# Moving the query casts of batches 2 to 7 from VectorE to GpSimd in a fused attention and feed-forward kernel

## The chip, the core and the metric

The kernel runs on one core of a Trainium2 chip. A core has TensorE (PE, matrix products), VectorE (DVE), ScalarE (ACT), GpSimd (POOL) and SyncE (SP). Each of them works through a queue of its own, in order, and waits on semaphores for the others. DMAs are issued from the queues of SP, POOL and ACT. The metric is the device time of one execution in microseconds (us), median over the runs.

## What is computed

A sliding-window attention (each position sees those at a distance of at most 32), then a feed-forward layer with the tanh form of GELU. The inputs are float32, 8 batches, 8 heads, 576 positions, 64 numbers per head; the feed-forward layer takes 4608 tokens of 512 numbers to 2048 and back.

```python
scores = scale * np.matmul(q, k.transpose(0, 1, 3, 2))
mask = np.abs(pos[:, None] - pos[None, :]) <= window
attn = softmax(np.where(mask, scores, -1e9))
x = (attn @ v).transpose(0, 2, 1, 3).reshape(B * S, H * D)
h = x @ w_in
out = gelu_tanh(h) @ w_out
```

(The softmax and the GELU are written out in the reference; they are named here to keep it short.)

## The kernel before

The attention of batch b and the feed-forward layer of the token tile t = b - 1 (512 tokens, nine tiles) run woven into each other. One tile goes like this. PE first computes the hidden columns: 16 columns of four 128x512 products each (`ffn_in`, L446), ScalarE applies the GELU to each (L454), and VectorE forms sums of them after every fourth column (`sums`, L487), since the second product is done with a scheme of seven block products for eight. Then PE runs the 112 products of the second layer (`ffn_out`, L542). Between these, at positions written by hand in the table `PLAN`, stand the steps of the attention of batch b: `s` is a score group (L354), one for each of the four head pairs and one for the tail positions; `m` the mask (VectorE, L369); `v` the weighting with V (L387); `x` the spreading of the result into the token buffer xT (VectorE, L411 and L417). The first score group stands after the sixth L542 product, the second after the 24th. PE takes all this in that order, without passing a step that waits.

The scheduling is by hand: each engine gets its instructions in the order in which the program emits them.

Queries and keys come as float32 with positions in rows, and the scores need them as float16 with the 64 numbers of a head in the partitions. For batches 0 and 1 this is done on PE. For batches 2 to 7, in the tiles t = 1 to 6, `cast_and_turn` does it, at the end of the first columns of the tile: VectorE casts the queries (`queries`, L310, four casts of 128x512, one per head pair) and SP issues one transposing DMA for them (L313, into QT); then for each head pair VectorE casts the keys (L318) and SP issues a transposing DMA (L319, into KT); then the same for the last 64 positions (L310 on 16 partitions and L313; L323 and L324). SP then issues the loads of the next batch's queries and keys (`load_qk`, L160 to L165). A score group of head pair p reads the whole of QT's pair p and KT's pair p.

GpSimd, in these tiles, only issues DMAs: the loads of V with a cast to float16 (`load_v`, L170 and L172: for batch 2 at the end of tile 0, for batch b + 1 behind the first `v` step in tile t), and the stores of the output rows (`store`, L503). Of a tile's stores, four are emitted after block product 5 (VectorE's L571) and seven in `ffn_last`, after VectorE's L580. `ffn_last` of a tile comes ahead of `cast_and_turn` of the next in the program.

The buffers that the change touches: the loaded queries `qr` (two), their tails `qt` (one), the casts `q16` and `qt16` (one each), QT and KT (two each).

Of the kernel before, what the change touches and what calls it, by code (L numbers as in the profile page):

```python
# [61 lines left out]
def kernel(  # L62
# [9 lines left out]
    nc = tc.nc  # L72
# [173 lines left out]
    def cast_open(b):  # L246
        halfs[b] = [hp.tile([128, NPAIR, 4, 2, 64], FP16, name="q16"),
                    hp.tile([128, NPAIR, 4, 2, 64], FP16, name="k16")]
        QTs[b] = ap_.tile([128, NPAIR, 4, 144], FP16, name="QT")
# [52 lines left out]
    def cast_and_turn(b):  # L302
        cast_open(b)
        q16, k16 = halfs[b]
        qr, kr, qt, kt = raws[b]
        qt16 = hp.tile([16, NPAIR, 4, 2, 64], FP16, name="qt16")
        kt16 = hp.tile([64, NPAIR, 2, 64], FP16, name="kt16")
        def queries(src, dst, p0, p1):
            for pr in range(NPAIR):
                nc.vector.tensor_copy(  # L310
                    dst[:, pr, :, :, :].rearrange("p j h d -> p h j d"),
                    src[:, 2 * pr:2 * pr + 2, :].rearrange("p h (j d) -> p h j d", j=4))
            nc.sync.dma_start_transpose(QTs[b].rearrange("d r j p -> d (r j) p")[:, :, p0:p1],  # L313
                                        dst.rearrange("p r j h d -> p (r j h d)"))

        queries(qr, q16, 0, 128)
        for pr in range(NPAIR):
            nc.vector.tensor_copy(k16[:, pr, :, :, :], kr[:, :, 2 * pr:2 * pr + 2, :])  # L318
            nc.sync.dma_start_transpose(  # L319
                KTs[b % 2][:, pr, 0:512].rearrange("d (c p) -> d c p", c=4),  # L320
                k16[:, pr, :, :, :].rearrange("p c h d -> p (c h d)"))
        queries(qt, qt16, 128, 144)
        nc.vector.tensor_copy(kt16.rearrange("p r h d -> p (r h d)"), kt.rearrange("p h d -> p (h d)"))  # L323
        nc.sync.dma_start_transpose(  # L324
            KTs[b % 2][:, :, 512:576], kt16.rearrange("p r h d -> p (r h d)"))
# [464 lines left out]
```

## Time and profile before

| What | Value |
|---|---|
| Median of 11 runs | 312.18 us (311.0 to 313.34) |
| The profiled execution | 311.7 us, its span 309.8 us |
| PE busy | 297.4 us (96%) |
| DVE busy | 198.4 us (64%) |
| ACT busy | 199.9 us (65%) |
| POOL busy | 102.2 us (33%) |
| Granted TensorE clock | 0.998 |

The span goes from the first to the last instruction in the trace; the execution's time has some 1.9 us around it. A row of a group of instructions gives line, engine, operation, what is written and read, shapes and count; behind the bar the busy time in us, the mean of one in ns, and the idle time of the engine just before, with what ended it. A row of a timeline gives start and length in us, engine, line and count; in brackets the idle time before and what ended it. "SPq" is SP's queue: the length there is that of issuing, and the data land later.

### The profile page before, as it was taken

To read this page: it belongs to the slowest core of one execution; us is meant where nothing else is said; L and a number is where in the kernel's file an instruction comes from. 1 tells how busy PE (TensorE), PEld (TensorE's weight loads), DVE (VectorE), ACT (ScalarE), POOL (GpSimd) and SP (SyncE) were. 2 spreads that over 40 slices of the span, in tenths; PEclk is the share of its full clock that TensorE was granted. 3 is DMA by queue.
4 is the path that set the end of the run, shared out by engine and by line. 5 is a ranking of instruction groups with operands and counts; after the bars stand their busy time and mean duration, and the time that the engine had idled before them with its cause. 6 is when DMAs were issued, how large, how long until landed. Compare 5 with 4: busy or idle time off the path is not lost.

```text
span 309.8 us, 6732 instructions
## 1 busy us (share of the span) xinstructions
PE 297.4 (96%) x2643; PEld 187.2 (60%) x2643; DVE 198.4 (64%) x453; ACT 199.9 (65%) x315; POOL 102.2 (33%) x158
## 2 busy tenths in 40 slices
PE   7888999999899999999999999999999999999993
PEld 2453545446684588548854785478647764784583
DVE  5763586669969477947785678666866643632451
ACT  1786477578577786768676777677768676706600
POOL 3557355192019210921094108510710061006000
PEclk9999999999999999999999999999999999999999
DMA  7999999999997998899779995999392022004013
GB/s 206 259 357 367 376 333 229 261 175 149 187 201 177 154 220 128 138 173 233 140 161 136 255 132 126 171 224 161 90 159 44 2 69 69 2 0 136 2 36 100
DMA packets 120061, 50.64 MB, mean 163 GB/s; under 512 B 101327, under 2 KB 113359, under 8 KB 120030
## 3 DMA queue, kind: packets, MB, share of 16 engines
q1 hardware_dynamic: 84329, 37.50, 58.9%
q0 software_dynamic: 34768, 11.54, 30.7%
q10 hardware_dynamic: 933, 1.18, 1.1%
q8 instruction: 20, 0.33, 0.5%
q14 instruction: 11, 0.09, 0.1%
HBM read 37.62 MB, written 9.44 MB: 152 GB/s over the span
## 4 chain that ended last, share of the span: by engine, by line
PE 71%; SPq 11%; DMA 11%; DVE 4%; issue 1%; POOL 0%; DVEq 0%
PE mm L542 30%; PE mm L446 20%; PE ph L446 12%; SPq L139 5%; PE ps_o L387 4%; DMA wst<-in_moe_w_in_dram 3%; PE ps_s L354 3%; DMA qr<-in_q_dram 3%; PE ps_d L387 2%; DMA KT<-k 2%; SPq L162 2%; DMA kr<-in_k_dram 2%; SPq L130 1%; SPq L185 1%; SPq L181 1%
## 5 line engine op out<-in xcount | busy, mean ns | idle before, releaser
L446 PEld LDWEIGHTS <-w_in 128*128 128x128 f16 x576 | 56.0, 98 | 66.4 <-POOL w_in L190 1.2
L446 PE MATMUL mm<-xT,w_in 128*128 128x512 f16 x352 | 86.3, 379 | 0.6 <-DVE xT L411 0.6
L503 POOL DMA_DIRECT2D out_dram<-y x77 | 45.2, 594 | 116.1 <-DVE y L571 115.4
L454 ACT ACTIVATE gT<-mm 128x512 f16<-128x512 f32 x88 | 52.4, 599 | 36.6 <-PE mm L446 36.6
L446 PE MATMUL ph<-xT,w_in 128*128 128x512 f16 x224 | 58.6, 379 | 0.3 <-POOL w_in L190 0.2
L487 DVE TENSOR_TENSOR s<-gT 128x512 f16<-128x512 f16 x64 | 26.9, 420 | 41.2 <-ACT gT L454 41.2
L542 PEld LDWEIGHTS <-s 128*128 128x128 f16 x512 | 48.6, 98 | 7.5
L360 ACT ACTIVATE pe<-ps_s 128x704 f16<-128x704 f32 x64 | 43.3, 727 | 9.1 <-PE ps_s L354 9.0
L542 PE MATMUL mm<-t,s 128*128 128x256 f16 x376 | 45.7, 273 | 0.0
L401 ACT ACTIVATE lt<-ps_d 128x480 f32<-128x480 f32 (+3 forms) x40 | 22.2, 556 | 31.0 <-PE ps_d L387 30.9
L454 ACT ACTIVATE gT<-ph 128x512 f16<-128x512 f32 x56 | 33.0, 599 | 13.8 <-PE ph L446 13.8
L542 PEld LDWEIGHTS <-gT 128*128 128x128 f16 x384 | 36.0, 98 | 7.3
L542 PE MATMUL mm<-w_out,gT 128*128 128x256 f16 x256 | 32.8, 273 | 0.0
L369 DVE TENSOR_TENSOR pe<-pe,mask 128x704 f16<-128x704 f16 x64 | 31.0, 521 | 1.7 <-ACT pe L360 1.5
L411 DVE TENSOR_TENSOR xT<-ps_o,lt 128x480 f16<-128x480 f32 (+5 forms) x38 | 20.2, 549 | 13.7 <-ACT lt L402 13.7
L387 PEld LDWEIGHTS <-V 128*64 128x64 f16 x336 | 17.9, 109 | 11.3 <-issue 4.7
L402 ACT ACTIVATE lt<-lt 128x480 f32<-128x480 f32 (+3 forms) x40 | 23.5, 587 | 1.3
L387 PE MATMUL ps_o<-pe,V 128*64 128x160 f16 (+2 forms) x244 | 21.8, 241 | 1.3 <-DMA V<-in_v_dram 0.7
L87 ACT ACT_TABLE_LOAD x17 | 21.8, 1283 | 1.1 <-PEq L774 0.8
L387 PE MATMUL ps_d<-pe,ones 128*64 128x192 f16 (+2 forms) x264 | 22.3, 235 | 0.0
L170 POOL DMA_DIRECT2D V<-in_v_dram x24 | 21.9, 940 | 0.0
L354 PE MATMUL ps_s<-QT,KT 64*128 64x192 f16 (+5 forms) x336 | 17.9, 227 | 1.2 <-DVE KT L290 1.1
(79 smaller groups left out, 296.2 us busy)
## 6 DMA issues: line engine op xcount, KB each, us to landing
kr<-in_k_dram SPq DMA_DIRECT2D x32, 256.0 KB, 6.8
qr<-in_q_dram SPq DMA_DIRECT2D x6, 1024.0 KB, 7.5
V<-in_v_dram POOLq DMA_DIRECT2D x30, 128.0 KB, 8.0
wst<-in_moe_w_in_dram SPq DMA_DIRECT2D x3, 1024.0 KB, 8.3
wst<-in_moe_w_out_dram SPq DMA_DIRECT2D x3, 1024.0 KB
qr<-in_q_dram SPq DMA_DIRECT2D x8, 256.0 KB
vr<-in_v_dram SPq DMA_DIRECT2D x16, 128.0 KB, 7.6
out_dram<-y POOLq DMA_DIRECT2D x24, 48.0 KB, 2.4
```

What stands on the lines that cost most here:

```text
L170: nc.gpsimd.dma_start(V[:, c, :, :], v[b, :, 128 * c:128 * c + 128, :].rearrange("h p d -> p h d"))
L354: nc.tensor.matmul(ps[:, h, off:off + 4 * n].rearrange("k (j p) -> k j p", j=4), KTs[b % 2][r0:r0 + 64, pr, k0:k0 + 128], QTs[b][r0:r0 + 6 ...
L360: nc.scalar.activation(pe, ps[:, :, 0:w], AF.Exp, scale=SCALE)
L369: nc.vector.tensor_tensor(pe, pe, m.rearrange("p (o w) -> p o w", o=1).broadcast_to(list(pe.shape)), op=ALU.mult)
L387: nc.tensor.matmul(bk[r0:r0 + 64, at:at + 4 * n].rearrange("d (j p) -> d j p", j=4)[:, :, p0 - q0:p1 - q0], V[:, c, 2 * pr + h, :] if w == ...
L401: nc.scalar.activation(lt[:, 0:n], d[:, 0:n], AF.Ln)
L402: nc.scalar.activation(lt[:, 0:n], lt[:, 0:n], AF.Exp, scale=-1.0)
L446: nc.tensor.matmul(ph, w_in16[:, dc, fc * 128:fc * 128 + 128], xT[:, dc, t * 512 % RING:t * 512 % RING + 512], start=(dc == 0), stop=(dc = ...
L454: nc.scalar.activation(gTs[t][:, fc, :], phs[fc], AF.Gelu_apprx_tanh)
L487: nc.vector.tensor_tensor(dst, x, y, op=op)
L503: (eng or turn_about[0] if t == NT - 1 else eng or nc.gpsimd).dma_start(out_v[b, j, q0 + p:q0 + p + e, cols], yo[m:m + e, cols])
L542: nc.tensor.matmul(pys["apart"][:, 0:256] if apart else py[:, blk, :], lhsT, wino[w][:, f, :], start=(new and i % (8 if one else 16) == 0) ...
```

## The change

In `cast_and_turn` the casts of the queries, those of the 512 first positions and those of the last 64, are emitted for GpSimd. The keys stay on VectorE. Nothing else is changed, and the order of the program is the same.

```diff
         def queries(src, dst, p0, p1):
             for pr in range(NPAIR):
-                nc.vector.tensor_copy(
+                nc.gpsimd.tensor_copy(
                     dst[:, pr, :, :, :].rearrange("p j h d -> p h j d"),
                     src[:, 2 * pr:2 * pr + 2, :].rearrange("p h (j d) -> p h j d", j=4))
             nc.sync.dma_start_transpose(QTs[b].rearrange("d r j p -> d (r j) p")[:, :, p0:p1],
                                         dst.rearrange("p r j h d -> p (r j h d)"))
```

It is called twice in each of six tiles, with four casts each time: 48 casts.

## The prediction, made before the change was built

> **What bounds the kernel now.** I read the page's busy shares first, then the time windows by stage, then the timelines of GpSimd (POOL), SyncE (SP) and TensorE (PE) around one batch change. The windows, one per token tile:
>
> ```profile
> core 0: us, PE busy (x) PEld busy (x) DVE busy (x) ACT busy (x) POOL busy (x), PEclk, DMA share, GB/s
> 60.00:93.00 33.00, 31.95 (x297) 20.82 (x296) 27.42 (x57) 23.04 (x38) 11.62 (x14) 1.00 1.54 179
> 93.00:125.00 32.00, 32.00 (x299) 20.97 (x298) 22.23 (x53) 23.57 (x38) 11.36 (x17) 1.00 1.20 167
> 188.70:220.50 31.80, 31.80 (x297) 20.83 (x296) 22.06 (x52) 23.37 (x38) 11.23 (x17) 1.00 1.12 164
> ```
>
> First column: length of the window; then busy time by engine. TensorE is busy in the whole of the tiles t = 2 to 6 and waits for nobody there. VectorE has about 10 us to spare in each. Only tile 1 (60 to 93 us) has holes in PE. So relief for VectorE is worth something in tile 1 alone, and anything that makes PE wait is paid in full.
>
> The groups of instructions give the price of the cast on each engine:
>
> ```profile
> L310 DVE CAST qt<-qt 16x512 f16<-16x512 f32 x24 | 9.2, 438 | 0.0
> L310 DVE CAST q<-qr 128x512 f16<-128x512 f32 x24 | 8.7, 423 | 0.0
> L253 POOL CAST q<-qr 128x512 f16<-128x512 f32 x7 | 4.5, 650 | 4.7 <-DMA qr<-in_q_dram 4.6
> ```
>
> The 48 casts that move are 17.9 us of VectorE time; the same shape took GpSimd 650 ns in the prologue.
>
> The timeline of GpSimd at the two batch changes that matter (start, length, line, count):
>
> ```profile
> 62.00 3.59 POOL L170 DMA_DIRECT2D V<-in_v_dram  x4
> 65.53 1.13 POOL L172 DMA_DIRECT2D V<-in_v_dram  x1
> ...
> 91.68 2.17 POOL L503 DMA_DIRECT2D out_dram<-y  x4 [14.72 <-DVE y L571]
> 94.09 4.53 POOL L503 DMA_DIRECT2D out_dram<-y  x7 [0.25 <-DVE y L580]
> 98.62 3.61 POOL L170 DMA_DIRECT2D V<-in_v_dram  x4
> ```
>
> That of SP, and PE's first two score groups of batch 3:
>
> ```profile
> 62.30 4.41 SPq L313 DMA_TRANSPOSE QT<-q  x1
> 66.81 6.32 SPq L319 DMA_TRANSPOSE KT<-k  x4
> ...
> 95.57 2.79 SPq L313 DMA_TRANSPOSE QT<-q  x1
> 98.46 6.57 SPq L319 DMA_TRANSPOSE KT<-k  x4
> ```
>
> ```profile
> 107.61 0.47 PE L354 MATMUL ps_s<-QT,KT 64*128 64x160 f16 x8
> ```
>
> What to see: GpSimd is not idle when the casts are due. It issues the eleven output stores of the tile just ended, the last seven only after VectorE's L580, and is done at 98.62; VectorE has finished the query casts at 95.5. The transpose of the queries (L313) heads SP's queue, and those of the keys (L319) stand behind it.
>
> **Part one: what is removed.** 24 x 423 + 24 x 438 ns = 20.7 us counted by means, 17.9 us busy without overlaps. In tiles 2 to 6 this is worth nothing (PE 32.00 of 32.00). In tile 1 the output stage, from PE's first L542 (73.80) to the next tile's first L446 (93.05), lasts 19.25 us against 17.99 in tile 2 (106.86 to 124.85). The 1.3 us difference are three waits: 0.32 for KT, 0.66 at 80.78 (the profile puts it down to a V load, but the spread L417 that frees the same PSUM bank ended at 80.63 on VectorE), 0.36 for xT. VectorE is busy without a break from 64.6 to 85; the tail casts leaving take 2.1 us out of that (those of qr end before a 2.4 us wait for kr and save nothing). Credit: 1.3 us at most, once.
>
> **Part two: how late the query transpose becomes.** GpSimd takes its queue in the order of the program: stores of the old tile, then the eight casts, then the V loads of the next batch. Tiles 2 to 6: stores end 3.05 us after today's issue of L313 (98.62 against 95.57; in the others 3.04, 3.05, 3.04, 3.05). The stores may get quicker: eleven took 6.7 to 6.8 us where VectorE casts beside them and 5.68 at 250.76, where it doesn't, so 0.516 each against 0.647 for the seven at 94.09. With 2.8 of 4.5 us of casts gone, 7 x 0.131 x 0.62 = 0.57 us. Then four casts: 4 x 0.65 = 2.6, and 0.07 for the semaphore, as today. Delay = 3.05 - 0.57 + 2.67 = 5.15 us. Bounds: 5.0 (casts at 0.613, the shortest usual) to 6.0 (stores no quicker, 0.72 as L190's on GpSimd).
>
> Here a rule of the Trainium skill bears on the price ("SBUF — State Buffer", section Terms): VectorE in a two-port mode and GpSimd take a shared port pair as an exclusive lock, and the loser blocks for a whole instruction. By it each of the four casts could wait for one of VectorE's sums (0.42 us), 1.7 us more. The row nearest, L190, has GpSimd at 0.71 to 0.72 beside busy VectorE against 0.61 alone: 0.1 per cast. I take the row; the rule's extra is in the upper end.
>
> Tile 1 is different: ahead of the casts stand the five V loads of batch 2, until 66.66. Delay = 66.66 + 2.67 - 62.30 = 7.03 us.
>
> **Part three: how much of that is covered.** From today's issue of L313 to score group 0 (it needs the queries and key pair 0) are 12.04 us in tile 2, and to group 1 (110.54) 14.97; in the other tiles 12.0 to 12.4 and 15.0 to 15.3. After the change 6.9 and 9.8 are left, in tile 1 5.3 and 8.3. The trace's DMA completion counts say when key pair 0 landed after the issue of L313: 12.3, 9.05, 9.84, 9.16, 8.75, 9.36 us in tiles 1 to 6; key pair 1: 13.5, 12.8, 13.0, 12.2, 10.9, 9.6. None fits. PE takes its queue in order, so it stands at the score group with all of L542 behind it.
>
> What these latencies will be is the main unknown. Upper end: as now, tile by tile. Then PE waits for the later of the two pairs, 3.0, 3.1, 2.3, 1.9, 2.4 us in tiles 2 to 6, and 7.0 in tile 1. Lower end: today the stores' packets run among the transposes, and after the change they are gone by then; the quickest query transpose landed 5.7 us after issue (tile 4), one key pair is 1.3 us more (the spacing on SP), so 7.0 and 8.3: PE waits 0.1 a tile and 1.7 in tile 1. I take the nearest undisturbed row, tile 5's 8.75 and 10.9 for all, because V loads (issued 2.6 us after L313 then, 3.05 now) still collide with the key transposes. Tiles 2 to 6: 8.75 - 6.9 = 1.86 each, 9.3 together; pair 1 (10.9 - 9.8 = 1.1) is then already paid. Tile 1: 8.75 - 5.3 = 3.4, less the credit of 1.3: 2.1.
>
> The other things moved: the four tail casts run behind the first four on GpSimd, ready before SP has issued the keys: nothing. V loads come some 5 us later; batch 3's landed by 82.8 and are read after 110: nothing. The next batch's q and k loads follow the transposes on SP and also slip by 5; the last key block landed at 93.5 for a cast at 95.4, so VectorE's key casts of batch 3 may wait some 2 us with the sums (L487) behind them, but the transpose of these keys stands behind that of the queries anyway: nothing, in later tiles the margin is over 5 us.
>
> Sum: 9.3 + 2.1 = 11.4 us. The profiled execution took 311.7 us (span 309.8), so 323.1; it lies 0.5 below the median of the runs, 312.18, which gives **323.6 us**.
>
> A second rule, "TensorE: Matmul & The Clock Gate", Part 1: after about 3.4 us without work PE's clock halves, and needs as long to come back. The row: PEclk is 9 in every slice, and the longest wait of PE in the trace is 1.3 us, so no row shows it. At 1.9 us a tile it costs nothing; with the upper end's 7.0 us in tile 1 it would add 1.7 us.
>
> **Rivals.** (a) The whole delay is passed on, latencies as today: 12.7 + 7.0 - 1.3 = 18.4, with the cold spell 20.1: 330.6 to 332.3. For it: the six latencies are measured with the same V loads; against it: the stores leave. Chance 0.2. (b) Transposes near their quickest: 0.5 + 0.4, up to 6 us: 313.1 to 318. For it: key pairs of tile 6, without V loads, landed 0.2 to 1.3 us apart. Chance 0.2. (c) Not slower: the transposes hide it all and VectorE's relief in tile 1 is kept. That decides at a latency of 6.9 us for pair 0 (5.3 in tile 1), against 8.75 at best today: 312.2 - 1.3 = 310.9. Chance 0.1, half of it within 0.3%. It is also what comes if GpSimd is given the casts ahead of the stores: then the delay is 4 x 0.23 = 0.9 us and lies within the 2 to 4 us of slack; but today's order on GpSimd is the program's. The forecast, 319 to 327: 0.5.
>
> About 0.3% (0.9 us) is what a measurement can tell from no change. Slower 0.9, same 0.05, faster 0.05. The range 314 to 332 leaves out (c) and the far end of (a).
>
> **What would show it.** Right: L313's transposes issue some 5 us later against the end of the stores' tile, after a GpSimd cast; PE has a wait of about 2 us before L354 in each of tiles 1 to 6, put down to KT or QT, none elsewhere; tiles lengthen from 31.8 to about 33.7; VectorE's busy time falls by 18 us and GpSimd's rises by about 31. Wrong: L313 issued before the stores; no wait at L354; waits of PE on s or xT, which would mean that port contention slows the sums instead.

## The result and the profile after

The changed kernel takes 317.14 us in the median of 12 runs (314.71 to 319.35), against 312.17 us of the kernel before; the ratio is 1.0157, with a 95% interval of 1.0137 to 1.0178. It is slower by 5.0 us. The forecast was 323.6, an increase of 11.4: the sign was right and the range holds the time, but the size is less than half of what was forecast.

The profiled execution took 317.17 us (span 315.5, against 309.8). Its windows, one per tile, cut where the tiles now begin:

```profile
core 0: us, PE busy (x) PEld busy (x) DVE busy (x) ACT busy (x) POOL busy (x), PEclk, DMA share, GB/s
61.30:98.00 36.70, 33.46 (x298) 21.74 (x297) 28.06 (x49) 23.23 (x38) 18.83 (x22) 0.95 1.43 159
98.00:130.60 32.60, 31.88 (x299) 20.82 (x297) 23.05 (x45) 23.50 (x38) 16.02 (x25) 1.00 1.24 163
194.20:226.00 31.80, 31.80 (x298) 20.78 (x297) 23.26 (x45) 23.38 (x38) 16.12 (x25) 1.00 1.11 166
```

Tile 1 now lasts 36.7 us with 3.2 us of holes in PE, and the granted clock falls to 0.95 in it; tile 2 lost 0.7 us. The tile at 194 us is as long as it was, and PE is busy in all of it. So the forecast wait of "about 2 us before L354 in each of tiles 1 to 6" came in tile 1, a little of it in tile 2, and nowhere else. PE's timeline at the first score group of batches 2, 3 and 4 (in brackets the wait):

```profile
78.79 0.74 PE L354 MATMUL ps_s<-QT,KT 64*128 64x160 f16 x8 [2.88 <-DMA KT<-k]
...
113.32 0.46 PE L354 MATMUL ps_s<-QT,KT 64*128 64x160 f16 x8 [0.72 <-DMA KT<-k]
...
145.12 0.47 PE L354 MATMUL ps_s<-QT,KT 64*128 64x160 f16 x8
```

GpSimd and SP at the two batch changes that the prediction shows:

```profile
66.74 0.94 POOL L172 DMA_DIRECT2D V<-in_v_dram  x1
67.61 4.96 POOL L310 CAST q<-qr 128x512 f16<-128x512 f32 x4
72.52 3.04 POOL L310 CAST qt<-qt 16x512 f16<-16x512 f32 x4
...
99.01 3.94 POOL L503 DMA_DIRECT2D out_dram<-y  x7 [0.24 <-DVE y L580]
102.94 2.48 POOL L310 CAST q<-qr 128x512 f16<-128x512 f32 x4
105.38 3.04 POOL L310 CAST qt<-qt 16x512 f16<-16x512 f32 x4
```

```profile
72.60 1.81 SPq L313 DMA_TRANSPOSE QT<-q  x1
74.51 1.87 SPq L319 DMA_TRANSPOSE KT<-k  x1
...
105.45 1.99 SPq L313 DMA_TRANSPOSE QT<-q  x1
107.54 1.65 SPq L319 DMA_TRANSPOSE KT<-k  x1
```

The casts stand behind the V loads in tile 1 and behind the stores in tile 2, and L313 is issued just after the fourth, as forecast. New to see: in tile 1 the four casts took 4.96 us, twice as long as in tile 2.

Where the 5.7 us of span went is read from PE's timeline, by the length of the second layer's stage (from the first L542 of a tile to the first L446 of the next). I call it the stage below. In tile 1 it lies between these rows, in the kernel before and then after:

```profile
73.80 0.82 PE L542 MATMUL mm<-w_out,gT 128*128 128x256 f16 x6
93.05 0.81 PE L446 MATMUL mm<-xT,w_in 128*128 128x512 f16 x3
```

```profile
75.09 0.82 PE L542 MATMUL mm<-w_out,gT 128*128 128x256 f16 x6
97.96 0.81 PE L446 MATMUL mm<-xT,w_in 128*128 128x512 f16 x3
```

| | tile 1 begins | stage of tile 1 | of tile 2 | of tiles 3 to 6 |
|---|---|---|---|---|
| before | 59.99 | 19.25 | 17.99 | 17.99 to 18.05 |
| after | 61.27 | 22.87 | 18.78 | 17.99 to 18.05 |

3.62 us in tile 1, 0.79 in tile 2, and 1.28 ahead of tile 1, where the programs are the same. The last I take for drift of the prologue from one execution to the next: tile 1 began between 60.1 and 61.5 in every kernel below, whether or not its casts had moved, and the 59.99 of before is the earliest of all. The part of the change in this trace is 4.4 us.

### The profile page after: what moved, and what is told of

Same layout as the page of the kernel before. It is cut to its first block, busy times and chain, and to the rows that moved or that the text cites. A ratio compares the mean times of both kernels' runs of the same rounds, so it can differ in the third digit from the quotient of the medians.

```text
span 315.5 us, 6732 instructions
## 1 busy us (share of the span) xinstructions
PE 300.0 (95%) x2643; PEld 188.5 (60%) x2643; DVE 205.1 (65%) x405; ACT 200.3 (64%) x315; POOL 134.9 (43%) x206
## 4 chain that ended last, share of the span: by engine, by line
PE 68%; DMA 13%; SPq 10%; DVE 6%; issue 1%; POOL 0%; ACT 0%; DVEq 0%
PE mm L542 30%; PE mm L446 17%; PE ph L446 10%; SPq L139 4%; PE ps_o L387 4%; PE ps_s L354 3%; DMA KT<-k 3%; DMA wst<-in_moe_w_in_dram 3%; DMA qr<-in_q_dram 3%; PE ps_d L387 3%; DVE s L487 2%; SPq L162 2%; DMA kr<-in_k_dram 2%; DMA vr<-in_v_dram 2%; DVE k L318 1%; SPq L181 1%
## 5 line engine op out<-in xcount | busy, mean ns | idle before, releaser
L446 PEld LDWEIGHTS <-w_in 128*128 128x128 f16 x576 | 56.0, 98 | 65.5 <-POOL w_in L190 0.7
L503 POOL DMA_DIRECT2D out_dram<-y x77 | 42.2, 555 | 111.2 <-DVE y L571 110.5
L446 PE MATMUL mm<-xT,w_in 128*128 128x512 f16 x352 | 86.3, 379 | 0.1
L446 PE MATMUL ph<-xT,w_in 128*128 128x512 f16 x224 | 58.5, 379 | 0.1
L487 DVE TENSOR_TENSOR s<-gT 128x512 f16<-128x512 f16 x64 | 34.7, 542 | 36.0 <-ACT gT L454 35.8
L542 PEld LDWEIGHTS <-s 128*128 128x128 f16 x512 | 48.6, 98 | 7.5
L542 PE MATMUL mm<-t,s 128*128 128x256 f16 x376 | 45.7, 273 | 0.0
L542 PEld LDWEIGHTS <-gT 128*128 128x128 f16 x384 | 36.4, 99 | 7.8
L542 PE MATMUL mm<-w_out,gT 128*128 128x256 f16 x256 | 33.7, 278 | 0.0
L369 DVE TENSOR_TENSOR pe<-pe,mask 128x704 f16<-128x704 f16 x64 | 32.1, 539 | 1.1 <-ACT pe L360 1.1
L387 PEld LDWEIGHTS <-V 128*64 128x64 f16 x336 | 18.3, 110 | 12.4 <-issue 5.8
L487 DVE TENSOR_TENSOR s<-s,gT 128x512 f16<-128x512 f16 x32 | 22.7, 710 | 1.1
L387 PE MATMUL ps_o<-pe,V 128*64 128x160 f16 (+2 forms) x244 | 21.7, 241 | 1.7 <-DVE pe L369 0.7
L354 PE MATMUL ps_s<-QT,KT 64*128 64x192 f16 (+5 forms) x336 | 18.2, 229 | 4.3 <-DMA KT<-k 3.6
L387 PE MATMUL ps_d<-pe,ones 128*64 128x192 f16 (+2 forms) x264 | 22.2, 235 | 0.0
```

Of the source, the lines that this page charges most:

```text
L354: nc.tensor.matmul(ps[:, h, off:off + 4 * n].rearrange("k (j p) -> k j p", j=4), KTs[b % 2][r0:r0 + 64, pr, k0:k0 + 128], QTs[b][r0:r0 + 6 ...
L369: nc.vector.tensor_tensor(pe, pe, m.rearrange("p (o w) -> p o w", o=1).broadcast_to(list(pe.shape)), op=ALU.mult)
L387: nc.tensor.matmul(bk[r0:r0 + 64, at:at + 4 * n].rearrange("d (j p) -> d j p", j=4)[:, :, p0 - q0:p1 - q0], V[:, c, 2 * pr + h, :] if w == ...
L446: nc.tensor.matmul(ph, w_in16[:, dc, fc * 128:fc * 128 + 128], xT[:, dc, t * 512 % RING:t * 512 % RING + 512], start=(dc == 0), stop=(dc = ...
L487: nc.vector.tensor_tensor(dst, x, y, op=op)
L503: (eng or turn_about[0] if t == NT - 1 else eng or nc.gpsimd).dma_start(out_v[b, j, q0 + p:q0 + p + e, cols], yo[m:m + e, cols])
```

## The experiments

Theory A: the whole loss is the wait for the transposes in tile 1 (with the slow clock that follows it), and a bit in tile 2; in tiles 3 to 6 the transposes land so much sooner after their issue that the delay is hidden. Theory B: the casts on GpSimd slow VectorE's sums by contention, in every tile alike. For B speaks the group of the sums on VectorE, here before and then after:

```profile
L487 DVE TENSOR_TENSOR s<-s,gT 128x512 f16<-128x512 f16 x32 | 13.6, 425 | 1.1
```

```profile
L487 DVE TENSOR_TENSOR s<-s,gT 128x512 f16<-128x512 f16 x32 | 22.7, 710 | 1.1
```

The stages in the profiles of all kernels, with the medians:

| kernel | median us | ratio to before, interval | stage of tile 1 | of tile 2 |
|---|---|---|---|---|
| from batch 3 on GpSimd | 313.02 | 1.0027 (1.0008 to 1.0047) | 18.72 | 18.19 |
| batch 2 alone on GpSimd | 316.25 | 1.0117 (1.0088 to 1.0146) | 23.61 | 17.99 |
| idle products | 315.76 | 1.0107 (1.0068 to 1.0145) | 21.47 | 17.99 |
| V loads behind the casts | 312.61 | 0.9999 (0.9977 to 1.0020) | 18.46 | 18.12 |
| stores behind the casts | 315.81 | 1.0104 (1.0065 to 1.0142) | 22.67 | 17.99 |
| long sums later | 314.55 | 1.0071 (1.0049 to 1.0093) | 20.31 | 19.15 |
| all early | 316.06 | 1.0118 (1.0090 to 1.0146) | 22.53 | 17.99 |
| batch 2 early | 315.66 | 1.0091 (1.0058 to 1.0123) | 22.29 | 17.99 |
| batch 2 early, V behind | 311.68 | 0.9980 (0.9967 to 0.9994) | 19.06 | 17.99 |
| all on GpSimd, V behind | 312.96 | 1.0016 (0.9999 to 1.0033) | 18.46 | 18.87 |
| seven stores left out | 313.79, one run | | 21.18 | 17.99 |
| no DMAs of GpSimd there | 312.98, one run | | 19.60 | 17.99 |

**Which batch costs it.** Two kernels halve the change:

```diff
-                nc.gpsimd.tensor_copy(
+                (nc.gpsimd if b > 2 else nc.vector).tensor_copy(
```

> Batch 2's query casts stay on VectorE, those of batches 3 to 7 are on GpSimd. Theory A (the loss is the wait for the transposes in tile 1, 3.6 us of it, and 0.8 in tile 2, while tiles 3 to 6 hide the delay): the time is that of before plus 0 to 0.9 us, 312.2 to 313.1, and TensorE has no wait over 0.8 us at L354. Theory B (port contention: VectorE's sums, 542 and 710 ns against 420, slow every tile alike): five sixths of the 5.0 us stay, about 316.3.

```diff
-                nc.gpsimd.tensor_copy(
+                (nc.gpsimd if b == 2 else nc.vector).tensor_copy(
```

> Only batch 2's query casts are on GpSimd. Theory A: the 3.6 us of tile 1 stay, and as the next loads slip, up to 0.8 more: 315.5 to 316.6; the clock drops to half for 3.4 us after the wait. Theory B: one sixth stays, about 313.0.

313.02 and 316.25, both where theory A has them. Five of six batches on GpSimd cost 0.7 us (in the profile 0.2 in the stage of tile 2 and 0.4 in that of tile 5), the one batch of tile 1 costs 3.9. Theory B falls: the sums are slower by the row above, but nobody waits for them, as VectorE had the time to spare. (In these tiles of after PE has three waits over 0.15 us: the two at L354, and 0.36 for xT, which before has too.)

**What the slow clock costs.** In the changed kernel the granted clock is halved in one stretch, from 78.6 to 82.0 us, right behind the wait in tile 1. The windows of that stretch (the three numbers at the end are PEclk, the DMA share and GB/s):

```profile
75.10:78.60 3.50, 0.81 (x7) 0.48 (x5) 3.43 (x9) 1.88 (x2) 3.50 (x5) 1.00 1.14 152
78.60:82.00 3.40, 3.21 (x33) 2.35 (x34) 1.27 (x4) 2.26 (x4) 1.30 (x2) 0.51 2.05 170
```

```diff
                 elif kind == "s":
+                    if t == 1 and g == 0:
+                        spin(14, 512)
                     score(*group(g))
```

> As after, with 14 idle products of 512 columns (3.0 us) on TensorE just ahead of the first score group of tile 1, into a spare bank, which compute nothing that is used. Theory A with the slow clock: they fill the wait, the granted clock stays at full, and the 3.4 us at half clock, worth up to 1.7 us, fall away: about 315.5. If the clock costs nothing: 317.1 or a little more.

315.76: 1.4 us less than after, and the stage of tile 1 is also 1.4 us shorter (22.87 to 21.47). The clock is full there:

```profile
75.30:79.00 3.70, 3.70 (x21) 1.85 (x19) 3.63 (x10) 1.88 (x2) 3.70 (x5) 1.00 0.74 86
79.00:83.00 4.00, 4.00 (x57) 3.17 (x57) 3.51 (x8) 2.90 (x5) 1.09 (x2) 1.00 2.15 157
```

But the products did not fill a wait here. In this execution the keys arrived later, VectorE's long sums (L471) therefore began behind the query casts, and the four casts took 3.03 us instead of 4.96:

```profile
67.80 3.03 POOL L310 CAST q<-qr 128x512 f16<-128x512 f32 x4
71.03 1.20 DVE L471 TENSOR_TENSOR t<-w_out 128x2048 f16<-128x2048 f16 x1
75.94 3.19 PE L215 MATMUL spin<-KT 128*128 128x512 f16 x14
```

Key pair 0 had landed at 75.9, about when score group 0 was due. So the idle products added their 3.0 us to a stage without the wait: 18.46 (the stage of the kernel with the V loads behind, below) and 3.0 are the 21.47. That a filled wait keeps the clock full is not shown by this run. The price of the slow clock comes out of the changed kernel itself: 22.87, less the 18.46 and the wait of 2.88, leaves 1.5 us. For batch 2 alone 23.61 - 18.46 - 3.54 leaves 1.6. PE does in 3.41 us at half clock what takes 1.7 at full clock, so 1.7 is the most that it could be.

**What stands ahead of the casts in tile 1.**

```diff
             load_table(gelu_set)
-            load_v(2)
...
                 cast_and_turn(b)
+                if b == 2:
+                    load_v(2)
```

> As after, with the five V loads of batch 2 behind that batch's query casts on GpSimd, so that these start about 4.4 us earlier. Theory A: the transpose of the queries is issued near 65.5 plus what the prologue drifts, the first score group of tile 1 waits under 0.7 us and the clock stays full: 312.5 to 313.5, with the 0.8 of tile 2 left; should V land late, PE waits at L387 instead. Theory B: no change, about 317.

312.61, not to be told from before, with all casts on GpSimd. PE doesn't wait at L354 in tile 1 and the clock stays full. Against the first L542 the query transpose is issued 7.1 us earlier than in after, not 4.4: the casts now also run while VectorE still waits for its keys, and take 2.28 us instead of 4.96:

```profile
62.55 2.28 POOL L310 CAST q<-qr 128x512 f16<-128x512 f32 x4
```

So the V loads ahead of the casts (4.4 us) and the slow casts behind them (2.7 us) were the price together.

**Why the casts took 4.96 us there.** In the changed kernel's timeline of VectorE, beside the third and fourth cast:

```profile
69.34 1.21 DVE L471 TENSOR_TENSOR t<-w_out 128x2048 f16<-128x2048 f16 x1
70.65 1.45 DVE L471 TENSOR_TENSOR t<-w_out,t 128x2048 f16<-128x2048 f16 x1
```

```diff
-        for dst, x, y in ((T1, B12, B11), (T2, B22, T1)):
-            nc.vector.tensor_tensor(dst, x, y, op=ALU.subtract)
...
-                    todo={17: (T3, B22, B12), 33: (T4, B21, T2)})
+                    todo={1: (T1, B12, B11), 2: (T2, B22, T1), 17: (T3, B22, B12), 33: (T4, B21, T2)})
```

> As after, with the first two sums of combine_w (L471, 1.2 us each on VectorE) emitted at products 1 and 2 of tile 1's second layer instead of beside the query casts. If these long two-input sums held GpSimd's casts (1.93 and 1.59 us for the third and fourth, against 0.61 alone), the four casts of tile 1 take about 3.0 us instead of 4.96, the transpose issues 2 us earlier, the wait at L354 falls from 2.9 to about 1 us and the clock stays full: 313.2 to 314.5. If the casts were slow for another reason: 317.1.

314.55 us, just past the upper edge. The four casts now take 3.03 us:

```profile
67.20 3.03 POOL L310 CAST q<-qr 128x512 f16<-128x512 f32 x4
```

and PE waits 0.98 us at L354 instead of 2.88, at full clock. Another 0.98 us of wait, at the products that need the sums now made later, is the experiment's own, and tile 2 waits 1.09 us at L354 instead of 0.72. The kernel with the idle products is a second witness: there the long sums met the tail casts instead, and the first four took 3.03 us with L471 in its old place. So whether the sums meet the query casts hangs on when the keys arrive, and this differs between executions of the same stage. How many of the 12 runs after the change were hit is not known; three profiles (after, batch 2 alone, stores behind the casts) have casts of 4.9 to 5.0 us.

**Why the transposes land sooner.** The trace's DMA completion counts give, for each tile, how long after the issue of L313 the queries and then key pair 0 had landed:

| kernel | tile 1 | 2 | 3 | 4 | 5 | 6 |
|---|---|---|---|---|---|---|
| before | 11.1, 12.3 | 6.8, 9.1 | 6.9, 9.8 | 5.7, 9.2 | 6.2, 8.8 | 8.9, 9.4 |
| after | 4.5, 6.1 | 4.4, 7.8 | 4.4, 6.0 | 4.4, 6.2 | 4.5, 6.0 | 4.4, 4.9 |
| stores behind | 4.5, 6.2 | 5.9, 7.5 | 8.3, 8.5 | 7.4, 7.8 | 7.5, 7.9 | 7.4, 7.6 |
| seven stores left out | 11.9, 13.0 | 9.1, 9.3 | 10.6, 10.8 | 8.4, 8.6 | 8.6, 8.8 | 6.1, 6.6 |
| no DMAs of GpSimd there | 11.8, 12.8 | 4.4, 5.1 | 5.4, 6.0 | 4.4, 4.9 | 4.4, 5.0 | 6.0, 6.6 |

After the change GpSimd issues no DMA from 2.5 us ahead of L313 (the casts fill that time) to 2.9 us behind it (the tail casts), and the queries land 4.4 to 4.5 us after issue in every tile. Three kernels ask whether it is that.

```diff
-                store(t, x, yo[:, x, :])
+                kept.append((t, x, yo[:, x, :]))
...
         queries(qr, q16, 0, 128)
+        while kept:
+            store(*kept.pop(0))
```

> As after, with the last seven stores of a tile emitted behind the query casts. In tiles 2 to 6 the query transpose is then issued some 4 us earlier than in after, within 1 us of before. Theory A with the stores' packets as cause of the long latencies of before: key pair 0 lands again 8.5 to 10 us after that issue (6.0 to 7.8 in after), and there is no wait at L354 in tiles 2 to 6; tile 1 is untouched, so the time is 0 to 0.8 us under after: 316.3 to 317.1. Rival (the latencies got shorter because VectorE has fewer casts, not because the stores had gone): they stay at 6 to 8 us.

With the stores back among the transposes the queries need 5.9 to 8.3 us again. Key pair 0 is at 7.5 to 8.5, short of the 8.5 to 10 that I had expected, and the transposes were issued 3.1 to 4.2 us earlier in the tile than after the change, so tile 2 loses its wait and the stage is 17.99. The time, 315.81, lies under the expected 316.3 to 317.1; its interval, 314.3 to 316.7, reaches into that.

```diff
         for x in range(2):
...
+            if 1 <= t <= 5:
+                continue
             if t < NT - 1:
                 store(t, x, yo[:, x, :])
```

> The kernel of before with the last seven stores of tiles 1 to 5 left out, so part of the output isn't written. If the stores' packets among the transposes make these slow, the query transpose of tile 6 (no V loads beside it) lands about 4.4 us after its issue and key pair 0 about 5 us after it, as in after; in before these were 8.9 and 9.4. If the stores have no part in it, 8.9 and 9.4 stay. The time is that of before, 311 to 313, since TensorE waits for none of this.

Tile 6 went from 8.9 and 9.4 to 6.1 and 6.6, not to 4.4 and 5: most of the way only. And in tiles 2 to 5 it got worse, which I hadn't foreseen: without the seven stores GpSimd reaches its V loads earlier, and these now run among the transposes. So it isn't the stores alone. (The time, 313.79, is above what I expected by its tile 1, in which this kernel is still that of before: four executions of that same stage took 18.72, 19.25, 19.60 and 21.18 us. With V loads among its transposes it is a fragile stage without the change too.) The last kernel takes the V loads of batches 4 to 7 out as well:

```diff
-                    if t and g < 0 and b + 1 < B:
+                    if t == 1 and g < 0:
                         load_v(b + 1)
```

> The kernel of before with the last seven stores of tiles 1 to 5 and the V loads of batches 4 to 7 left out, so part of the output isn't written and part is computed from a stale V. If it is GpSimd's own DMAs among the transposes that make these slow in before, the query transposes of tiles 3 to 6 land 4.3 to 4.6 us after their issue and key pair 0 4.9 to 6.2 us after it, as in after. If VectorE's query casts have a part in it: 5.7 to 8.9 and 8.8 to 9.8, as in before.

4.4 and 4.9 to 5.1 us in tiles 2, 4 and 5, with VectorE's query casts where they were in before; but 5.4 and 6.0 in tile 3 and 6.0 and 6.6 in tile 6, outside what I had expected for the queries. So most of the long latencies come from GpSimd's DMAs beside the transposes, and VectorE's casts don't stand in the way of 4.4. SP's own issue of L313 shows the same in this kernel: 1.84 us in tile 4 against 3.25 in before.

```profile
160.50 1.84 SPq L313 DMA_TRANSPOSE QT<-q  x1
```

The traces hold one more thing for tiles 3 and 6. Between the issue of L313 and its landing a packet of the queue that the profile calls "instruction" ran there. Tiles 2, 4 and 5 have none. This is the row of tile 3 (packets, MB, share of 16 engines from 128.7 to 134.1 us):

```profile
q8 instruction: 1, 0.02, 1.2%
```

Tile 6 of the kernel with seven stores left out (6.1) and tiles 2 and 5 of that with the idle products (5.9 and 6.0) have such a packet too, and no tile of after has one. No run tests whether it is the cause.

**Whether it can be had for less.** Batch 2's queries have landed near 58 us, and GpSimd waits for the store of tile 0 until 61. Two kernels cast them there, the second with the other batches early as well. Of the first:

```diff
         queries(qr, q16, 0, 128)
+        queries(qt, qt16, 128, 144)
...
-        queries(qt, qt16, 128, 144)
...
                         load_qk(2)
+                        turn_queries(2, nc.gpsimd)
```

> Only batch 2's query casts are on GpSimd, early, in its idle time behind the load of the queries; those of batches 3 to 7 stay on VectorE. Both theories: the waits of tile 1 (1.3 us in before) shrink by 0.7 to 1.3: 310.9 to 311.5.

> All query casts on GpSimd, but early: batch 2's behind the load of its queries in tile 0, the others' and their transposes in the tile ahead, before product 88 of its second layer. Theory A: no wait at L354 at all, and VectorE's relief in tile 1 is kept: 310.9 to 311.6. Theory B: the casts fall beside masks and spreads on VectorE, which TensorE waits for, and slow these: 313 or more.

315.66 and 316.06: both expectations missed. I had moved the tails' transpose along with the rest, ahead of the keys on SP. In the first of the two:

```profile
62.54 3.50 SPq L313 DMA_TRANSPOSE QT<-q  x1
70.19 1.15 SPq L313 DMA_TRANSPOSE QT<-qt  x1
71.43 5.75 SPq L325 DMA_TRANSPOSE KT<-k  x4
```

The tail casts on GpSimd waited for their load until 66.0, were then held up by the long sums and ended at 70.2; the keys, cast by 67.8, stood behind them on SP until 71.4. A wait went into a queue that I had not walked through. In tiles 2 to 6 of both the stage is 18.0, as in before: in the second, which has the casts in the middle of a tile, they cost nothing there.

The mended kernel casts only the first 512 positions of batch 2 early, leaves the tails behind the keys (on GpSimd), and puts the V loads of batch 2 behind these:

```diff
                         load_qk(2)
+                        cast_open(2)
+                        queries(2, raws[2][0], halfs[2][0], 0, 128, nc.gpsimd)
...
                 cast_and_turn(b)
+                if b == 2:
+                    load_v(2)
```

> Batch 2's first query casts on GpSimd in its idle time behind their load, the tails behind the keys as in before, the V loads of batch 2 behind the tails; batches 3 to 7 on VectorE. Theory A: no wait at L354 in tile 1, whose second layer lasts 18.0 to 18.6 us; 310.9 to 312.2.

311.68 us, ratio 0.9980 (0.9967 to 0.9994), the best of all and a gain of 0.2%, close to what can be told from nothing. In tile 1 key pair 0 landed 6.1 us after the issue of the query transpose, and PE doesn't wait for it. The stage is 19.06 all the same, longer than the 18.0 to 18.6 expected: PE waits 0.57 us for a spread on VectorE, as it did in before (0.66 at L387). With the other batches on GpSimd too, in the place of the change:

> As the one with batch 2 early and V behind, with the query casts of batches 3 to 7 on GpSimd in the place of the change. Theory A: these cost nothing where the transposes land 6 us after their issue: within 0.5 us of that kernel. Rival (port contention costs something in every tile): 0.5 to 1.5 us more.

312.96, 1.3 us more, where I had expected at most 0.5. By the profile the loss isn't spread over the tiles, as port contention would have it: tiles 3 to 6 are as long as in before, and 0.88 us lie in tile 2's stage, where key pairs land late at score groups, as in after. That was to be expected from after's own 0.79. But tile 1's stage is 0.60 us shorter in turn, and tile 1 begins 0.77 later, ahead of which the programs are the same; so this pair of profiles does not fully account for the 1.3 us between the medians. Why the keys land later in tile 2 than in tiles 3 to 5 of the same kernel (7.8 us against 6.0 to 6.2 in after) stays open.

## Why the prediction was right in sign and wrong in size

*What bounds the kernel, and what relief is worth.* Right in the main. VectorE gave up 17.9 us of casts, and no tile from 2 to 6 became shorter. (Its busy time rose all the same, from 198.4 to 205.1 us: an instruction that waits for GpSimd counts as busy (a sum of 0.42 us lasted 2.17, see the end), so the fall by 18 us that I named as a sign did not come.) The credit for tile 1 was too high: 0.32 us "for KT" is the idle time of the weight load ahead of the score group, and PE itself came 0.11 us late there (0.86 behind its first L542, 0.75 in tile 2). The 0.36 for xT is also in the stage of 18.46 of the kernel with the V loads behind. What there was to gain is 19.25 - 18.46, 0.8 us instead of 1.3.

*The delay of the query transpose.* Against the first L542 of the same tile, L313 moved by 5.0, 4.9, 5.0, 5.0 and 5.4 us in tiles 2 to 6; forecast 5.15. Both terms held: the stores got quicker (seven in 3.94 us instead of 4.53), and four casts took 2.48 us in tiles 2 to 5. In tile 1 it moved by 9.0 us where 7.03 was forecast. The term that failed there is 4 x 0.65 = 2.6 for the casts: 4.96 measured. There I had set the Trainium skill's rule of the exclusive port pair ("SBUF — State Buffer", Terms) against the row of L190 and taken the row. The rule would have been the better guide. VectorE's sums of 1.2 us beside them (L471) held two casts for 1.93 and 1.59 us, and with these sums moved away four casts took 3.03. I had priced the rule with the sums of 0.42 us that follow, and not looked at what VectorE does in just those microseconds. Nor was the meeting certain: in the kernel with the idle products the same casts missed the long sums.

*How much is covered.* This is the step that made the size wrong: "I take the nearest undisturbed row, tile 5's 8.75 and 10.9 for all". Measured: key pair 0 after 7.8, 6.0, 6.2, 6.0 and 4.9 us in tiles 2 to 6, against a budget of 6.9. Four of five fit, and the forecast 9.3 us became 0.8. Tile 5 was not undisturbed: the stores and V loads that GpSimd issued around it had lengthened it too, as the kernel without these DMAs shows (4.4 and 5.0 in the same tile). I had written down the reason in the lower end, that the stores would be gone by then, and estimated 7.0 from it, close to what came; and then weighted it too little because V loads "still collide with the key transposes". They do, but behind the queries: without V loads (the last kernel, tiles 4 and 5) pair 0 landed after 4.9 to 5.0 us and pair 1 after 6.2, with them (after) at 6.0 to 6.2 and 8.3 to 8.8.

*Tile 1.* Forecast a wait of 3.4 less a credit of 1.3. Measured a wait of 2.88: the delay was 2.0 us longer than forecast and the latency 2.6 us shorter (6.1 against 8.75), so two errors nearly cancelled, by luck. The stage's 3.62 us are the wait of 2.88, less the 0.11 and the 0.66 (at L387) that before had lost, and 1.5 of slow clock. The 0.36 for xT is in both.

*The clock.* I put the cold spell in the upper end alone, at 7 us of wait, by the Trainium skill's rule of 3.4 us without work ("TensorE: Matmul & The Clock Gate", Part 1). It came with a wait of 2.88 us, and cost 1.5 us. The duration of the spell, 3.41 us, is what the page says; the wait that brings it on can be shorter, down to 2.54 us here (batch 2 early). The half clock begins 2.7 to 3.9 us after the wait has begun, in four of five kernels when PE is already at work again. I had also written that no row of before shows the rule. One does. PE's last product ends at 305.0, and the clock (the first of the last three numbers) is down in what follows:

```profile
306.00:309.80 3.80, 0.00 (x0) 0.00 (x0) 0.00 (x0) 0.00 (x0) 0.00 (x0) 0.85 0.27 80
```

A mean of 0.85 in 3.8 us is half clock in the last 1.1, from 308.7 on, 3.7 us after the last product.

*The rivals.* (b), transposes near their quickest, is what happened in tiles 2 to 6, and I gave it 0.2; its time, 313.1 to 318, holds the result. Its own tile 1 was too cheap.

## What to carry to other kernels

A step that is moved to an idle engine is not free there: walk its new queue for what stands ahead of it at that moment, and look at what the engine that it gets in the way of does in the same microseconds. A latency read off a trace belongs to the traffic around it; if the change moves the issue past that traffic, the old latency is not the new one, and the one row that looks clean should be checked for what was in flight. And where one tile differs from the rest, cost it on its own: here one batch of six made most of the loss.

## What the runs showed of the hardware

- A transposing DMA of 128x2048 float16 landed 4.4 to 4.5 us after its issue in every tile of after, where GpSimd issued no DMA from 2.5 us before it to 2.9 us behind it, and needed 5.7 to 11.9 us with GpSimd's stores or casting loads beside it. In five tiles with few or none of these, but one packet of the instruction queue beside it, it took 5.4 to 6.1.
- GpSimd and VectorE held each other up. Where both had a row of work they took turns: a cast of 0.62 us lasted 0.80 and a sum 0.82 instead of 0.42. One sum waited through three casts in a row and lasted 2.17:

```profile
102.78 2.17 DVE L487 TENSOR_TENSOR s<-s,gT 128x512 f16<-128x512 f16 x1
104.88 0.82 DVE L487 TENSOR_TENSOR s<-gT 128x512 f16<-128x512 f16 x1
```

- Casting 16 partitions took GpSimd as long as casting 128 (787 and 790 ns in the means), as on VectorE (438 and 423 ns).
- PE's clock was halved for 3.41 us around or behind single waits of 2.54 to 3.54 us (five kernels), and stayed full behind waits of 0.98 and 1.64 us.
